# Two prices of a plan, and the order of 531 TensorE tasks, in a float32 attention and mixture-of-experts kernel

## The chip, the cores and the metric

One NeuronCore of one Trainium2 chip. The metric is device time in microseconds (us) of one execution. The kernel before takes 580.03 us, the median of 3 runs (580.02 to 580.44).

## The reference

Eight batches, eight heads, 576 positions, 64 wide: block-causal attention (blocks of 64), its output x goes into four experts, each with its own q, k, v projections (512 to 64) and causal attention, an output projection, and a gate that keeps two of the four.

```python
# attention, per batch and head
scores = q @ k.T / 8;  mask where block(i) < block(j);  attn = softmax(scores);  x = attn @ v
# experts, per batch
logits = x @ w_gate;  w = softmax over the top 2 of 4
for e in range(4):
    q, k, v = x @ wq[e], x @ wk[e], x @ wv[e]
    a = softmax(causal(q @ k.T / 8))
    out += gate[e] * (a @ v @ wo[e])
```

## The kernel before, in words

The work is cut into 48 slots: per batch four pairs of heads of the first attention ("A") and two pairs of experts ("M"), 12.5 us apart in the plan (`TSLOT`). Each slot does for its two heads, with keys and queries on 64 partitions each:

- **scores** (`f_s` in `add_attention`): query tiles of 128 rows against as many keys as the mask lets through, widths 192, 320, 448, 576 (`WID`). `ORDER` groups them in three tasks: the widest tile 3 (with a 64x64 corner), tiles 0 and 1, tile 2. Most are three products of a high and a low part (`hl`, `lo`); tile 0 and the first batch multiply plain float32 (`raw`, `mops`). The tasks of tiles 0, 1 and of tile 2 are called narrow here, that of tile 3 wide.
- row minimum of the negated, masked scores on DVE (`f_m`), exp with a running sum on ACT (`f_e`).
- **transposes** of the exps (`f_t`, 14, 15 or 16 per task), copied from PSUM by ACT or DVE into `eTa` (tiles 0, 1) and `eTb` (tiles 2, 3) (`f_v`).
- **eT times v** (`f_av`, 24 or 32 matmuls as the trace counts them), scaled with the reciprocals of the sums (`f_p1`), split into a high and a low part (`f_p2`, `f_p3`).

Beside the slots stand the **full** products: q and k of the experts (`add_qk`), v (`add_v`), the output projection (`add_out`). On TensorE (PE) these four kinds use the array in three ways. The plan marks each PE task with a mode: F for the full products (128x128), C for eT times v (128x64), S for scores and T for transposes (both 64x128, `TILING` "H").

What sets the order: the kernel does not rely on a scheduler but plans itself (`Plan.run`). Every task has a cost, dependencies and buffers. The plan plays the five queues (PE, ACT, DVE, POOL, SP) forward in its own clock and emits each task when its turn comes. PE's tasks come strictly in the order of the table `LINE`, a permutation of the 531 PE tasks; a task that is not ready keeps PE waiting. The other engines take the ready task with the lowest number in the table `KEYS`, and some tasks (copies, splits) go to whichever of ACT, DVE and POOL is free. `PRICE` is what the plan adds to a PE task when the mode changes ("SF" from S to F), and `c_s` in `add_attention` is what it takes a score task to last. So with a given `LINE` the prices do not order PE; they move the plan's clock of PE, and with it what the other engines find ready.

Of the kernel before, what the change touches and what calls it, by code (L numbers as in the profile page):

```python
# [58 lines left out]
    -61.05, 72.88, -304.49, 285.38, 197.97, 308.44, -90, -485.75, -398.95, -311.49, -310.46, -226.23, -303.95,  # L59
    -200.29, -34.36, -109.87, -30.06, -772.41, 406.92, 36.99, -152.28, -87.06, 7.08, -98.82, 506.04, 1.62, 144.12,  # L60
    -49.87, 59.34, -401.18, 304.55, 589.82, -639.65, -37.72, 51.33, 51.13, 363.43, -16.73, -65.89, 69.77, 71.38,
    -371.59, 575.7, 149.12, -52.5, 104.96, 107.99, -1.27, 338.51, 239.38, -211.47, 124.56, 122.39, -297.31, 280.07,
    443.51, 233.11, 147.49, 81.63, 12.96, 1067.18, 161.48, 784.65, 161.42, 125.87, -195.35, 725.34, 807.9, -217.87,
    164.5, 141.44, 175.16, 781.63, 677.59, 325.44, 163.12, 140.52, 144.51, 440.22, 268.84, -137.83, 201.27, 173.02,
    245.23, 629.28, 442.61, 545.51, 202.32, 269.87, 173.82, 832.33, -48.65, 499.89, 229.38, 195.56, 624.52, 150.18,
    707.74, -57.93, 261.4, 295.79, -255.42, 325.91, 465.42, -305.64, 289.89, 257.36, 257.93, 1202.64, 49.62, 413.63,
    301.23, 296.29, -8.39, 1198.8, 76.81, 224.38, 306.63, 303.26, 535.45, 953.46, 368.95, 582.51, 325.55, 295.98,
    566.34, 713.9, -18.75, -179.96, 357.63, 358.03, 216.69, 733.92, 406.86, 396.51, 391.78, 372.27, -114.52, 562.3,
    652.52, 305.73, 395.02, 342.63, 556.86, 344.09, 662.77, 447.36, 425.58, 400.46, 722.61, 650.31, 592.99, 244.69,
    455.55, 501.82, 523.83, 758.38, 354.59, 317.8, 567.08, 439.03, 70.97, 1094.19, -324.07, 311.7, 595.2, 522.52,  # L70
    314, 531.55, 124.8, 629.88, 471.62, 520.83, 451.03, 1089.28, 1137.64, 795.01, 765.66, 707.37, 477.57, 1225.45,
    -221.62, 764.62, 598.95, -76.75, 113.9, 240.74, -125.38, -108.02, 404.04, 93.98, -349.15, -30.71, -12.22,
    -140.33, -142.11, 6.12, -438.84, -44.69, 364.95, 34.38, 352.96, 61.78, 351.19, 110.73, 5.01, 757.03, -6.95,
    359.21, 201.49, 1.84, -54.25, 483.22, -739.78, -731.32, 7.17, 255.2, -85.56, 415.17, -499.83, 20.32, -281.08,
    186.92, -9.52, -412.56, -28, -25.13, 491.02, 6.62, -368.72, 413.41, 17.8, -980.05, -328.7, -497.05, -449.07,
    69.73, -166.75, -214.9, 26.69, 125.25, 497.09, 242.37, 20.29, 258.64, -36.7, 432.07, 170.76, 11.09, -277.3,
    271.15, -748.81, 581.22, 23.95, 894.06, 241.77, -424.41, -274.26, 36.21, 212.12, -455.4, 231.78, -274.77, 20.91,
    -194.25, 52.79, -25.53, -371.82, 262.65, -26.69, -273.2, -337.99, 142.42, -257.02, 228.08, -130.15, -390.41,
    52.82, 98.9, 885.98, -46.42, 35.39, -29.22, 100.36, -431.26, 404.1, 22.61, -20.89, 71.79, -77.48, 53.08, 24.92,
    548.27, 43.24, -5.98, -509.78, 33.61, 208.79, 192.46, -68.15, 373.75, 7.71, 181.82, -201.58, 31.77, -169.86,  # L80
    348.99, 7.75, 43.39, 264.75, -279.03, 489.2, -193.62, 187.58, 123.51, 52.03, 394.77, -1008.75, -262.95, 58.43,
    -6.54, -604.46, 155.8, -166.41, 32.92, -563.72, -421.41, 295.9, 78.7, 36.85, 695.62, 68.35, 462.77, 504.63,
    32.59, 70.25, 641.61, 219.12, 107.13, 19.31, 131.63, 280.91, 13.26, -242.14, 251.73, 24.01, -717.93, -49.16,
    20.04, -133.98, 215.52, 580.48, -20.65, 59.42, -46.59, 305.54, 243.5, 105.29, -509.23, -516.01, 60.21, -25.78,
    59.3, 358.94, 36.45, -57.58, 74.48, 47.05, 308.04, -206.22, 957.49, 561.1, 64.27, 23.46, 219.54, -583.14,
    -352.66, 33.3, 234.83, -114.24, 35.96, -36.27, 62.05, 66.29, 27.38, -93.48, -671.09, 248.87, -73.25, 180.17,
    -151.19, 82.16, 695.44, 798.54, 364.87, 85.48, 456.72, 301.84, 571.42, 98.78, 69.55, -90.33, 300.55, 18.48,
    1035.48, 22.07, 143.29, 275.43, 196.22, -144.5, 69.53, 503.83, -521.13, 158.9, 520.48, 63.86, 227.15, -629.77,
    25.79, -77.04, 364.92, 49.61, 769.8, 576.6, -693.16, 32.64, -127.69, 345.55, -588.48, 87.18, -233.43, 454.17,
    -515.68, 108.56, -318.55, 263.11, -12.2, 884.88, -43.3, -139.58, 32.01, 277.78, -330.98, -21.7, 567.38, 70.38,  # L90
    8.99, -14.06, 550.12, 90.72, -424.31, -79.85, 75.31, 653.46, 61.48, 364.25, 75.19, 709.07, 76.28, -24.9, 79.85,
    429.96, -603.55, 434.76, 563.52, 346.37, -904.62, -424.27, 217.54, 208.46, -33.4, 323.46, 794.21, 307.74,
    -575.64, -93.77, -160.66, -264.36, -24.47, -372, 593.97, 132.98, -766.42, 80.06, 156.45, 84.68, -5.9, -598.24,
    -67.41, 1106.11, 90.26, -113.18, 83.63, 180.77, 482.69, 99.87, 294.41, 53.86, 149.08, 298.76, -64.86, -891.13,
    81.25, 170.92, -658.3, -250.1, 337.52, 81.14, 602.58, 499.67, 318.97, 487.72, 73.66, 573.01, 415.62, 81.04,
    -71.18, 832.82, 46.33, 255.81, 368.96, -207.19, 51.95, 52.91, 182.3, 159.13, 215.44, 100.54, 286.85, 567.36,
    480.88, 115.39, -433.72, 20.08, -359.31, 81.17, 211.56, -224.8, -265.4, 276.02, 86.93, 588.8, 796.85, 236.19,
    8.45, 93.86, 305.75, 447.42, 506.63, -212.19, 54.29, 198.19, 631.11, 50.3, -339.7, 179.38, 78.24, -43.31,
    -236.77, -530.02, -149.28, 236.07, 446.91, 239.47, 128.01, 104.9, -502.35, 86.41, 111.82, -196.67, 62.74, 34.46,
    -175.69, 97.86, 211.82, 131.16, -117.5, -621.65, 109.31, 310.73, -8.42, -299.88, 614.46, 105.04, 208.76, 828,  # L100
    150.18, -258.73, 96.27, 244.6, 418.51, 60.84, 419.07, -319.32, 104.95, -235.03, 231.9, 555.33, -163.95, -172.06,
    -103.02, -106.94, 139.89, 323.89, -114.19, -336.01, 125.66, -580.49, -690.47, 385.08, -53.84, 115.29, -248.33,
    -1087.38, -27.82, 430.69, 122.89, -244.35, 1060.62, 4.9, 320.44, 125.84, -281.29, -87.32, 704.44, 132.13,
    116.99, -134.72, -527.81, 104.13, -316.36, -254.53, 69.33, 378.26, 89.26, -228.7, 592.26, 360.76, 113.77,
    -177.01, 292.79, 138.4, -717.17, -252.74, 550.47, 143.5, 622.23, 58.38, -301.1, 133.13, -375.99, -24.11, 128.06,
# [182 lines left out]
PRICE = {"FC": 100, "FS": 160, "FT": 85, "CF": 155, "CS": 175, "CT": 148, "SF": 155, "SC": 153, "ST": 0,  # L288
         "TF": 135, "TC": 105, "TS": 8}
# [1072 lines left out]
```

## Time and profile before

| | |
|---|---|
| median of 3 runs | 580.03 us (580.02 to 580.44) |
| profiled execution | 579.71 us, its span 577.9 us |
| PE busy | 566.2 us, 98% of the span |
| DVE, ACT, POOL busy | 467.3, 432.7, 211.0 us (81, 75, 37%) |
| granted TensorE clock | 1.000 |
| DMA | 113 GB/s mean |

The span runs from the first to the last instruction; the profiled execution's own time is 1.8 us longer. "Idle before" is the time in which an engine had nothing running, and what ended it. A busy PE is not the same as a PE at its peak: matmuls are pipelined, and a change of mode lengthens the distance between two tasks without showing as idle time. So the text below measures a PE task by the distance from its first matmul's start to the first start of the next task.

### The profile page before, as it was taken

The numbers are of one execution on the slowest core, as the hardware profiler recorded it, in microseconds if no ns is written. First come the engines' busy times: TensorE is split into PE (matmuls) and PEld (weight loads), VectorE is DVE, ScalarE is ACT, GpSimd is POOL, SyncE is SP. The second block draws the span as 40 slices with busy tenths as digits, with TensorE's granted clock in tenths as the row PEclk, the third lists the DMA queues.
The fourth block names the chain that finished last, engine by engine and source line by source line (L and its number), as shares of the span: only waits on it lengthen the run. The fifth ranks groups of instructions, "written<-read, shape, count | busy, mean of one in ns | idle before, by whom it ended". The sixth has DMA issues, their size and how long they took to land.

```text
span 577.9 us, 19767 instructions
## 1 busy us (share of the span) xinstructions
PE 566.2 (98%) x7794; PEld 525.3 (91%) x7794; DVE 467.3 (81%) x1630; ACT 432.7 (75%) x1363; POOL 211.0 (37%) x330
## 2 busy tenths in 40 slices
PE   7899999999999999999999999999999999999996
PEld 5689999999999989999999999999999999999984
DVE  6999789798978789888877878878898889774851
ACT  5888787888767787677877868768778787665743
POOL 2475236434442253322333516164542434120011
PEclk9999999999999999999999999999999999999999
DMA  6555234322543144422173315343253230301042
GB/s 232 170 197 203 94 123 152 105 67 82 166 163 85 64 121 128 140 83 86 62 240 108 105 41 169 98 143 107 65 183 124 85 105 5 118 4 45 2 173 91
DMA packets 29853, 65.51 MB, mean 113 GB/s; under 512 B 9664, under 2 KB 10176, under 8 KB 29760
## 3 DMA queue, kind: packets, MB, share of 16 engines
q1 hardware_dynamic: 24224, 54.51, 29.6%
q10 hardware_dynamic: 5536, 9.73, 4.8%
q8 instruction: 61, 1.00, 0.7%
q14 instruction: 32, 0.26, 0.2%
HBM read 54.01 MB, written 10.22 MB: 111 GB/s over the span
## 4 chain that ended last, share of the span: by engine, by line
PE 95%; DVE 3%; ACT 1%; issue 0%; POOL 0%; ACTq 0%; DVEq 0%; POOLq 0%
PE bank L325 95%; DVE bank L325 1%; DVE eTb L325 1%; ACT e L325 0%; DVE eTa L325 0%; DVE nm L325 0%; DVE x L325 0%; ACT ob L325 0%; DVE r L325 0%; ACTq L325 0%; POOL id masks.py:199 0%; POOL id masks.py:197 0%; DVE rT L325 0%; DVEq L325 0%; POOLq masks.py:199 0%
## 5 line engine op out<-in xcount | busy, mean ns | idle before, releaser
L325 ACT ACTIVATE e<-bank,nm 128x320 f32<-128x320 f32 (+3 forms) x384 | 218.7, 580 | 27.9 <-DVE nm L325 24.2
L325 DVE CUSTOM_DVE_ANT_0 bank<-bank,mask_a 64x64 f32<-64x64 f32 (+4 forms) x320 | 154.6, 505 | 15.3 <-PE bank L325 8.6
L325 PE MATMUL bank<-x,wh 128*128 128x320 f32 (+1 forms) x512 | 105.7, 301 | 0.0
L325 PEld LDWEIGHTS bank<-id,e 64*128 64x128 f32 x2112 | 86.5, 140 | 14.0 <-issue 5.0
L325 PE MATMUL bank<-id,e 64*128 64x64 f32 x2112 | 96.2, 226 | 1.7 <-ACT e L325 1.6
L325 POOL TENSOR_TENSOR lo<-raw,hl 128x320 fp32r<-128x320 f32 x77 | 65.6, 878 | 78.6 <-ACT hl L325 73.1
L325 PEld LDWEIGHTS bank<-x,wh 128*128 128x128 f32 x512 | 82.0, 188 | 4.0 <-issue 2.7
L325 DVE CUSTOM_DVE_ANT_0 bank<-bank,mask_c 64x64 f32<-64x64 f32 (+4 forms) x160 | 77.4, 506 | 7.3 <-PE bank L325 3.7
L325 PE MATMUL bank<-hl,lo 64*128 64x320 f32 (+2 forms) x352 | 79.9, 380 | 0.4 <-DVE eTb L325 0.4
L325 ACT ACTIVATION_READ_ACCUMULATOR e<-bank,nm 128x1 f32 x384 | 78.5, 204 | 0.0
L325 PE MATMUL bank<-x,wl 128*128 128x256 f32 (+1 forms) x256 | 75.7, 296 | 0.0
L325 ACT COPY eTb<-bank 128x512 f32<-128x512 f32 (+1 forms) x111 | 58.9, 557 | 19.4 <-PE bank L325 18.7
L325 PE MATMUL bank<-hl 64*128 64x320 f32 (+2 forms) x352 | 68.0, 313 | 0.0
L325 PE MATMUL bank<-lo,hl 64*128 64x320 f32 (+2 forms) x352 | 67.7, 313 | 0.0
L325 DVE DVE_READ_ACCUMULATOR2_ANT nm<- 128x1 f32 (+1 forms) x480 | 67.0, 139 | 0.0
L325 PEld LDWEIGHTS bank<-eTb,va 128*64 128x64 f32 x1024 | 59.6, 137 | 3.7 <-issue 2.1
L325 PE MATMUL bank<-eTb,va 128*64 128x128 f32 (+2 forms) x1024 | 62.8, 275 | 0.0
L325 DVE TENSOR_TENSOR x<-bank,rs 128x256 f32<-128x256 f32 (+1 forms) x144 | 46.3, 352 | 17.8 <-PE bank L325 15.1
L325 PE MATMUL bank<-wh,x 128*128 128x260 f32 x288 | 59.2, 289 | 0.0
L325 DVE COPY eTb<-bank 128x512 f32<-128x512 f32 (+1 forms) x81 | 51.7, 654 | 9.2 <-PE bank L325 8.3
L325 PEld LDWEIGHTS bank<-wh,x 128*128 128x128 f32 x288 | 46.9, 188 | 2.9 <-issue 1.4
L325 POOL TENSOR_TENSOR x<-x,x 128x256 fp32r<-128x256 f32 (+1 forms) x43 | 34.9, 814 | 36.8 <-ACT x L325 18.6
(116 smaller groups left out, 1170.4 us busy)
## 6 DMA issues: line engine op xcount, KB each, us to landing
va<-in_v_dram SPq DMA_DIRECT2D x32, 576.0 KB
raw<-in_qk_dram SPq DMA_DIRECT2D x31, 576.0 KB
rs<-dr SPq DMA_DIRECT2D x96, 144.0 KB
out_dram<-ob ACTq DMA_DIRECT2D x32, 256.0 KB
raw<-in_w_dram SPq DMA_DIRECT2D x4, 386.0 KB
out_dram<-ob ACTq DMA_DIRECT2D x8, 128.0 KB
dr<-rT SPq DMA_DIRECT2D x48, 16.0 KB
raw<-in_wo_dram SPq DMA_DIRECT2D x1, 512.0 KB
```

What stands on the lines that cost most here:

```text
L325: r = f(*args, **kwargs)
```

## The change

Both tables are new: `KEYS` (2619 numbers) for the other engines, `LINE` for PE. 269 of the 531 places in `LINE` hold another task than before; of those 148 moved by one place, 67 by two, the farthest by 23. Every task's own instructions are the same, the number of PE instructions too. 79 tasks go from DVE to ACT, 77 from ACT to DVE, 58 from DVE to POOL or back, 37 from ACT to POOL or back; ACT has 730 tasks (721 before), DVE 889 (897), POOL 303 (304).

```diff
 KEYS = [
-    -61.05, 72.88, -304.49, 285.38, 197.97, 308.44, -90, -485.75, -398.95, -311.49, -310.46, -226.23, -303.95,
+    162.95, 160.21, -395.85, 276.68, 82.54, 260.02, -90, -520.61, -409.21, -275.21, -352.21, -239.63, -265.52,
...
 LINE = [
-    0, 2, 1, 3, 4, 12, 5, 11, 6, 10, 7, 20, 9, 18, 15, 19, 13, 14, 8, 23, 22, 28, 26, 21, 16, 27, 17, 25, 31, 30,
+    0, 1, 2, 3, 4, 12, 11, 5, 6, 10, 7, 20, 9, 18, 15, 19, 14, 8, 28, 23, 13, 22, 26, 21, 27, 17, 16, 25, 29, 31,
...
-PRICE = {"FC": 100, "FS": 160, "FT": 85, "CF": 155, "CS": 175, "CT": 148, "SF": 155, "SC": 153, "ST": 0,
+PRICE = {"FC": 100, "FS": 160, "FT": 85, "CF": 155, "CS": 175, "CT": 148, "SF": 200, "SC": 185, "ST": 0,
          "TF": 135, "TC": 105, "TS": 8}
...
             c_s = sum(4 * WID[t] / 2.4 + 10 if hl is None or t == 0 else 3 * (WID[t] / 2.24 + (8 if last else 4)) for t in ts_)
-            c_s += 174 * last + 25 + (32 if ts_[0] == 0 else 18) + 40 * (hl is None)
+            c_s += 174 * last + (25 if last else -20) + (32 if ts_[0] == 0 else 18) + 40 * (hl is None)
```

How often one mode follows another in PE's order, from its 32nd task on (the first 31 are the start, which the prediction takes by itself):

| from, to | F to C | F to S | F to T | C to F | C to S | C to T | S to F | S to C | S to T | T to F | T to C | T to S | no change |
|---|---|---|---|---|---|---|---|---|---|---|---|---|---|
| before | 5 | 3 | 42 | 4 | 12 | 20 | 32 | 15 | 41 | 15 | 16 | 72 | 222 |
| changed | 3 | 5 | 43 | 6 | 14 | 19 | 25 | 14 | 43 | 21 | 22 | 62 | 222 |

All seven of the S to F that are gone left a narrow score task.

Three places. The first is ACT's order in the first pair of heads (exps read a bank, `e_99` is tile 3, `e_97` and `e_98` tile 2 of this pair and the next; numbers are buffers). Before:

```order
6 L325 ACTIVATE el_101,ssum_82<-bank_146,nm 64x64
7 L325 ACTIVATE e_99,ssum_82<-bank_146,nm 128x576
8 L325 ACTIVATE el_101,ssum_82<-bank_147,nm 64x64
9 L325 ACTIVATE e_99,ssum_82<-bank_147,nm 128x576
10 L325 ACTIVATE e_97,ssum_82<-bank_144,nm 128x448 x2
11 L325 ACTIVATE e_98,ssum_83<-bank_145,nm 128x448
12 L325 ACTIVATE r_136<-ssum_82,eps 128x10
13 L325 ACTIVATE e_98,ssum_83<-bank_145,nm 128x448
```

Changed:

```order
8 L325 ACTIVATE el_101,ssum_82<-bank_146,nm 64x64
9 L325 ACTIVATE e_99,ssum_82<-bank_146,nm 128x576
10 L325 ACTIVATE e_97,ssum_82<-bank_144,nm 128x448
11 L325 ACTIVATE e_97,ssum_82<-bank_145,nm 128x448
12 L325 ACTIVATE e_98,ssum_83<-bank_144,nm 128x448
13 L325 ACTIVATE e_98,ssum_83<-bank_145,nm 128x448
14 L325 ACTIVATE el_101,ssum_82<-bank_147,nm 64x64
15 L325 ACTIVATE e_99,ssum_82<-bank_147,nm 128x576
16 L325 ACTIVATE r_136<-ssum_82,eps 128x10
```

The second head's exp of tile 3 now stands behind four exps of width 448, where it stood before them. DVE's minima change in the same way.

The second is PE's order at the same place (`raw_73` and `raw_74` are q and k of the first two pairs, `id` marks transposes). Before:

```order
8 L325 MATMUL bank_146<-raw_73 128x64
9 L325 MATMUL bank_147<-raw_73 128x64
10 L325 MATMUL bank_144<-raw_73 128x448 x2
11 L325 MATMUL bank_145<-raw_74 128x448 x2
12 L325 MATMUL bank_146<-id_65,e_99 128x64 x16
13 L325 MATMUL bank_147<-raw_74 128x192 x2
14 L325 MATMUL bank_147<-raw_74 128x320 x2
15 L325 MATMUL bank_144<-id_65,e_95 128x64 x4
```

Changed:

```order
12 L325 MATMUL bank_144<-raw_73 128x448
13 L325 MATMUL bank_145<-raw_73 128x448
14 L325 MATMUL bank_144<-raw_74 128x448
15 L325 MATMUL bank_145<-raw_74 128x448
16 L325 MATMUL bank_146<-raw_74 128x192 x2
17 L325 MATMUL bank_146<-raw_74 128x320 x2
18 L325 MATMUL bank_144<-id_65,e_99 128x64 x16
19 L325 MATMUL bank_145<-id_65,e_95 128x64 x4
```

The scores of the next pair's tiles 0 and 1 (`raw_74`, widths 192 and 320) now come ahead of the 16 transposes of `e_99` instead of behind them.

The third is PE's order in the middle of the program (tasks 232 to 236 of 531): the end of a wide score task, a narrow one of width 448 (`hl_77`), and eT times v (`eTa`, `eTb`). Before:

```order
2183 L325 MATMUL bank_147<-raw_74 128x64
2184 L325 MATMUL bank_144<-raw_74 128x64
2185 L325 MATMUL bank_145<-hl_77,lo_79 128x448
2186 L325 MATMUL bank_146<-hl_77,lo_79 128x448
2187 L325 MATMUL bank_145<-hl_77 128x448
2188 L325 MATMUL bank_146<-hl_77 128x448
2189 L325 MATMUL bank_145<-lo_79,hl_77 128x448
2190 L325 MATMUL bank_146<-lo_79,hl_77 128x448
2191 L325 MATMUL bank_146<-eTa_104,vz 64x64 x2
2192 L325 MATMUL bank_146<-eTa_104,vm 64x256
2193 L325 MATMUL bank_146<-eTa_104,vm 64x2x64
```

Changed:

```order
2214 L325 MATMUL bank_146<-raw_75 128x64
2215 L325 MATMUL bank_147<-raw_75 128x64
2216 L325 MATMUL bank_145<-id_65,e_99 128x64 x16
2217 L325 MATMUL bank_144<-eTa_103,vz 64x64 x2
2218 L325 MATMUL bank_144<-eTa_103,vm 64x256
2219 L325 MATMUL bank_144<-eTa_103,vm 64x2x64
2220 L325 MATMUL bank_144<-eTa_103,vm 64x64
2221 L325 MATMUL bank_144<-eTa_103,vz 64x2x64
2222 L325 MATMUL bank_144<-eTa_103,vm 64x128
2223 L325 MATMUL bank_144<-eTa_103,vz 64x64 x5
2224 L325 MATMUL bank_144<-hl_77,lo_79 128x448
2225 L325 MATMUL bank_145<-hl_77,lo_79 128x448
```

Before, the narrow scores followed the wide ones and then came both products with v. Now 16 transposes follow the wide scores (they stood ahead of them), and the narrow scores stand between the two products with v: C to S and S to C once more, S to S and C to C once less.

## Rows read from the trace of the kernel before

**Rows 1.** the page: busy time, share of the span and number of instructions by engine; the shares of the chain that ended last.

```profile
PE 566.2 (98%) x7794; PEld 525.3 (91%) x7794; DVE 467.3 (81%) x1630; ACT 432.7 (75%) x1363; POOL 211.0 (37%) x330
...
PE 95%; DVE 3%; ACT 1%; issue 0%; POOL 0%; ACTq 0%; DVEq 0%; POOLq 0%
```

**Rows 2.** busy time by engine in stretches of the execution: start and end, length, then for each engine its busy time and its instructions, the granted TensorE clock in parts of full speed, DMA share, GB/s.

```profile
40.00:300.00 260.00, 259.97 (x3646) 243.74 (x3644) 222.24 (x775) 203.05 (x643) 104.02 (x160) 1.00 0.36 118
300.00:560.00 260.00, 260.00 (x3574) 243.87 (x3572) 208.71 (x725) 193.88 (x612) 86.85 (x133) 1.00 0.30 93
```

**Rows 3.** who waited for whom, PE's rows alone, from 0 to 40 us: total wait, times, longest. (From 40 us to the end the same view has no row for PE.)

```profile
PE bank L325 <- ACT e L325: 2.8, 5, 1.1
PE bank L325 <- POOL id masks.py:199: 1.4, 1, 1.4
```

**Rows 4.** timeline of PE, 424.5 to 440 us (start, length, engine, line, operation, out<-in, tile, count; in brackets idle time before): the first row of each of some tasks and the row that begins the next.

```profile
427.10 0.39 PE L325 MATMUL bank<-woh,y 128*128 128x512 f32 x1
...
428.49 0.28 PE L325 MATMUL bank<-wh,x 128*128 128x260 f32 x1
...
430.79 0.59 PE L325 MATMUL bank<-id,e 64*128 64x64 f32 x11
...
431.19 0.46 PE L325 MATMUL bank<-hl,lo 64*128 64x448 f32 x1
...
433.70 0.40 PE L325 MATMUL bank<-woh,y 128*128 128x512 f32 x1
...
435.18 0.41 PE L325 MATMUL bank<-hl,lo 64*128 64x320 f32 x2
...
438.64 1.22 PE L325 MATMUL bank<-eTa,va 128*64 128x64 f32 x24
439.79 0.40 PE L325 MATMUL bank<-id,e 64*128 64x64 f32 x6
```

**Rows 5.** timeline of PE, 474 to 484.8 us, same columns.

```profile
478.82 0.22 PE L325 MATMUL bank<-eTa,va 128*64 128x64 f32 x1
...
479.82 0.22 PE L325 MATMUL bank<-eTa,vz 128*64 128x64 f32 x1
...
483.19 0.36 PE L325 MATMUL bank<-hl,lo 64*128 64x448 f32 x1
...
483.80 0.55 PE L325 MATMUL bank<-hl,lo 64*128 64x448 f32 x2
...
484.68 0.41 PE L325 MATMUL bank<-x,wh 128*128 128x320 f32 x1
```

**Rows 6.** timeline of PE, 490.4 to 503.9 us, same columns.

```profile
497.83 0.44 PE L325 MATMUL bank<-hl,lo 64*128 64x448 f32 x1
...
498.51 0.48 PE L325 MATMUL bank<-mops 64*128 64x192 f32 x3
...
499.27 0.54 PE L325 MATMUL bank<-id,e 64*128 64x64 f32 x10
...
499.98 0.50 PE L325 MATMUL bank<-woh,y 128*128 128x512 f32 x1
...
501.47 0.28 PE L325 MATMUL bank<-wh,x 128*128 128x260 f32 x1
```

**Rows 7.** timeline of PE, 392.4 to 395.8 us, same columns.

```profile
393.24 0.50 PE L325 MATMUL bank<-hl,lo 64*128 64x448 f32 x2
...
393.85 0.54 PE L325 MATMUL bank<-id,e 64*128 64x64 f32 x10
...
394.57 0.33 PE L325 MATMUL bank<-eTa,vz 128*64 128x64 f32 x4
...
395.62 0.41 PE L325 MATMUL bank<-eTb,vm 128*64 128x256 f32 x3
```

**Rows 8.** timeline of PE, 83 to 84 us, same columns.

```profile
83.35 0.54 PE L325 MATMUL bank<-id,e 64*128 64x64 f32 x12
...
83.94 0.41 PE L325 MATMUL bank<-x,wh 128*128 128x320 f32 x1
```

**Rows 9.** timeline of PE, 341.3 to 343 us and 528.9 to 532 us, same columns.

```profile
341.47 0.59 PE L325 MATMUL bank<-id,e 64*128 64x64 f32 x12
...
341.93 0.39 PE L325 MATMUL bank<-hl,lo 64*128 64x320 f32 x1
...
529.70 0.47 PE L325 MATMUL bank<-hl,lo 64*128 64x448 f32 x2
...
530.41 0.31 PE L325 MATMUL bank<-hl,lo 64*128 64x320 f32 x2
```

**Rows 10.** timeline of ACT and PE in the first attention pair, 0 to 20 us, same columns.

```profile
10.14 0.31 ACT L325 ACTIVATE el<-bank,nm 64x64 f32<-64x64 f32 x1
...
11.16 0.62 ACT L325 ACTIVATE e<-bank,nm 128x448 f32<-128x448 f32 x1
...
11.31 0.72 PE L325 MATMUL bank<-id,e 64*128 64x64 f32 x16 [0.99 <-ACT e L325]
...
11.77 0.62 ACT L325 ACTIVATE e<-bank,nm 128x448 f32<-128x448 f32 x1
...
11.87 1.08 PE L325 MATMUL bank<-raw 64*128 64x192 f32 x8
...
12.79 0.54 PE L325 MATMUL bank<-id,e 64*128 64x64 f32 x12
```

426 rows, old and new, of tables (KEYS, LINE) are left out of this document.

## The prediction

> **What bounds the kernel.** I read the page first: PE is busy 98% of the span, and the chain that ended last lies on PE for 95% of it [rows 1]. Then the busy times by stretch: from 40 to 560 us PE is never without work (519.97 of 520 us) at the full granted clock, while DVE and ACT are at 75 to 85% [rows 2]. Then who waited for whom: PE waits only in the first 40 us, 6.3 us in all by that view, of which 1.4 us is the wait for the identity matrix and 2.8 us for exps [rows 3]. So past the start no transfer and no other engine sets the pace, and PE's work does not change: the same tasks with the same instructions. What can change there is the distance between tasks where the mode changes. The last views are therefore PE's timeline at such places [rows 4 to 9] and the start [rows 10].
>
> **What a change of mode costs.** I take the distance from a task's first matmul to the next task's first, for one kind of task in different company, and split each price into what the task that leaves is lengthened by and what the task that enters is.
>
> - F: an output projection between two F tasks lasts 1.39 us (427.10 to 428.49) [rows 4]. Ahead of scores it lasts 1.48 (433.70 to 435.18) [rows 4]: leaving costs 0.09. Behind transposes 1.49 (499.98 to 501.47) [rows 6]: entering costs 0.10.
> - T: 15 transposes between two score tasks last 0.40 (430.79 to 431.19) [rows 4]. Ahead of F or C 0.71 [rows 6] and 0.72 [rows 7], but also 0.59 (83.35 to 83.94) [rows 8]: leaving costs 0.19 to 0.32, and I take 0.25, the middle. Behind F 0.46 [rows 9]: entering costs 0.06; behind C the same is assumed.
> - S: a score task of width 448 between two S lasts 0.61 (483.19 to 483.80), ahead of F 0.88 [rows 5]: leaving costs 0.27, and to C the same is assumed. Ahead of T 0.61 (393.24 to 393.85) [rows 7]: free. Behind T 0.68 [rows 6]: entering 0.07. Behind F 0.71 [rows 9]: 0.10, from C the same.
> - C: 24 products with v between C tasks last 1.00 [rows 5], behind T 1.05 [rows 7], ahead of T 1.15 [rows 4]: entering 0.05, leaving 0.15.
>
> The sums of leaving and entering: S to F 0.37, S to C 0.32, T to F 0.35, T to C 0.30, F to S 0.19, F to T 0.15, C to S 0.25, C to T 0.21, C to F 0.25, F to C 0.14, T to S 0.07, S to T 0.
>
> **What the new order adds from the 32nd PE task on** (the table of the change, changed minus before): S to F -7, that is -2.59 us; S to C -1, -0.32; F to C -2, -0.28; C to T -1, -0.21; T to S -10, -0.70. Against it T to F +6, +2.10; T to C +6, +1.80; C to S +2, +0.50; C to F +2, +0.50; F to S +2, +0.38; F to T +1, +0.15. Together +1.33 us. The new prices make leaving S dearer in the plan, and the order does leave from T instead, but the trace gives T nearly the same price, and four more stretches of S and T are opened and closed. The uncertain piece is T's leaving: at 0.19 on all twelve the sum is +0.6, at 0.32 it is +2.1. The third place of the order is one such case: products with v cut in two by a narrow score task.
>
> The rule of the Trainium skill for this, page "TensorEngine Tiling (Array Packing)", section "Key Properties" under "Tiling Modes", is that changing the tiling mode drains TensorE, while another tile in the same mode does not. By it all changes between F, C and S or T would cost alike and T to S nothing; that is the fourth rival below. The trace agrees that T to S is nearly free, and not that the others are equal: 0.14 to 0.37 us.
>
> **The start.** ACT takes the second head's exp of tile 3 after four exps of width 448 instead of before. Such an exp takes 0.61 us of ACT (11.16 to 11.77), so it begins 2.4 us later than at 10.14, and the 16 transposes that wait for it, at 11.31 before with 0.99 us of idle PE ahead of them, would come at about 13.7 [rows 10]. Into that wait PE now puts the next pair's scores of tiles 0 and 1, 0.92 us (11.87 to 12.79) [rows 10]. So the 15 transposes behind begin at 13.7 + 0.6 = 14.3 in place of 12.79: +1.5 us. What is late next are the copies of those transposes, and the next scores that need their banks. Much of the delay is given back, since of PE's waits some 3.3 us still follow in the start (6.3 less 1.4, 0.99 and 0.6 for a transfer), and in each of them a late PE waits less: ACT paces this stretch, and its exps are the same. I take +0.2 us; bounds +1.5 (nothing given back) and -1.0 (the wait of 0.99 is filled and the exp is not late).
>
> **At nothing.** The moves between ACT, DVE and POOL (ACT nine tasks more, DVE eight fewer, POOL one fewer): covered by PE, which never waits for them past 40 us [rows 2, 3]; if the cover is gone, see the fifth rival. SP's queue: loads of v change places at the start, with the products that use them in nearly the same places on PE; no PE wait on a load of v is in the trace, and a late one would be part of the +1.5 above. The end: the last copies and stores on ACT are in the same order, and only two half projections of PE's last three change places: nothing.
>
> **Sum.** 1.33 + 0.2, about +1.5 us. The profiled execution took 579.71 us, with a span of 577.9 and 1.8 around it, which I leave as it is; it lies 0.32 below the median of the runs. The sum put on the execution gives 581.2, on the median 580.03, which is what will be compared, **581.5 us**. Its own range, with T's price and some of the start, is 580.4 to 582.4.
>
> **Rivals.** I call no change what is within 0.2%, 1.16 us, about what a measurement of this kernel can tell.
>
> 1. The forecast, +1.5 us: chance 0.38.
> 2. Faster: the start. PE loses 4.9 us there after the identity. If the new order fills the 0.99 us and half of the other 3.9, it gains 2.9 us, and with +1.3 for the modes the time is 578.4. It decides from a gain of 2.5 us in the start. For it: all of PE's idle time that an order can still win lies there, and scores are indeed put into the wait. Against it: the exp that is waited for is put off by 2.4 us. Chance 0.22.
> 3. The change does not do what its prices say: T is as cheap to leave as the cheap rows (0.19), the start comes out even, +0.6 us, 580.6: no change. For it: 0.59 [rows 8] is as real as 0.71. Chance 0.20.
> 4. Each change of tiling costs the same. From the 32nd task on there are 172 of them instead of 164; the mean of the prices above over the 164 is 0.26 us, so +2.1, and with the start 582.3. Against it: leaving C or F is cheaper than leaving S or T in the rows. Chance 0.12.
> 5. New waits in the middle: a transpose task moved ahead meets an exp that is not there yet. PE's waits for exps in the start are 2.8 us in five, 0.6 each [rows 3]; three such give +1.8 on top, 583.3. Against it: before has none in 520 us with ACT and DVE this busy [rows 2]. Chance 0.08.
>
> **How the numbers follow.** The forecast's range falls on both sides of +1.16: of its 0.38, 0.25 is slower and 0.13 no change. Rivals 4 and 5 are slower (0.20), rival 3 is no change but for 0.02 on either side (0.16), rival 2 is faster but for 0.01. So slower 0.47, no change 0.30, faster 0.23. The range from 578.5 to 583.4 leaves out about half of rival 2 and half of rival 5, with a little beyond: under 2 in 10.
>
> **What would show it.** Right: from 40 us on PE has no idle time as before, yet it needs over a microsecond more for the same tasks; tasks of transposes ahead of F or C last 0.6 to 0.7 us, and there are more of them; the 16 transposes of the first tile 3 begin near 13.7 us with over 2 us of idle PE ahead, and by the 32nd task the delay is a few tenths. Wrong: PE's total wait in the first 40 us well below 6.3 us (rival 2); a PE row in the waits after 40 us (rival 5); transposes ahead of F or C mostly at 0.6 us (rival 3).

## The result, and the profile after

The changed kernel takes 583.56 us, the median of 6 runs (582.95 to 586.59), against 580.02 (579.23 to 580.49, 6 runs) for the kernel before: a ratio of 1.0074, 95% interval 1.0049 to 1.0100. That is 3.5 us slower where 1.5 was forecast, and just outside the range (583.4). The profiled execution took 583.92 us, its span is 582.1 us. All of the 4.2 us between the spans can be followed on PE, task by task, because both orders hold the same tasks. One execution below, of the kernel with the prices alone, was slow (713.59 us at a granted clock of 0.725) and is left out of its figures.

PE's waits from 0 to 40 us in the profile after, against [rows 3]:

```profile
PE bank L325 <- ACT e L325: 3.7, 4, 2.3
PE bank L325 <- POOL id masks.py:199: 2.1, 1, 2.1
PE bank L325 <- DVE eTb L325: 0.6, 1, 0.6
PE bank L325 <- ACT eTb L325: 0.2, 1, 0.2
```

The sum is hardly larger (6.6 us, before 6.3), but it lies in other places: 0.7 more for the identity and one wait of 2.3 for an exp. The stretches of [rows 2], after:

```profile
40.00:300.00 260.00, 258.52 (x3608) 243.38 (x3605) 219.32 (x766) 203.48 (x644) 107.21 (x162) 1.00 0.36 117
300.00:560.00 260.00, 259.77 (x3599) 243.50 (x3598) 210.60 (x736) 194.83 (x611) 86.48 (x134) 1.00 0.29 92
```

Past 40 us PE now has 1.48 us of idle time in one place and 0.2 in another, where it had none. PE's timeline in the start and at that place (idle time before in brackets), against [rows 10]:

```profile
10.62 1.13 PE L325 MATMUL bank<-raw 64*128 64x192 f32 x8 [0.84 <-ACT e L325]
14.08 1.63 PE L325 MATMUL bank<-id,e 64*128 64x64 f32 x28 [2.33 <-ACT e L325]
...
15.95 2.26 PE L325 MATMUL bank<-raw 64*128 64x320 f32 x12
...
19.76 2.00 PE L325 MATMUL bank<-eTb,va 128*64 128x256 f32 x32 [0.25 <-ACT eTb L325]
...
41.95 0.41 PE L325 MATMUL bank<-hl,lo 64*128 64x320 f32 x2 [1.48 <-DVE eTa L325]
```

The 16 transposes of the first tile 3 start at 14.08 (before: 11.31) behind 2.33 us of idle PE, as the prediction said. What it did not say stands in the granted clock, the third column from the right in this view by stretches of 1 us:

```profile
13.00:14.00 1.00, 0.00 (x0) 0.00 (x0) 0.93 (x5) 1.00 (x5) 0.92 (x2) 1.00 0.00 0
14.00:15.00 1.00, 0.92 (x20) 0.92 (x22) 0.93 (x6) 0.33 (x2) 1.00 (x2) 0.65 0.00 0
15.00:16.00 1.00, 0.97 (x19) 0.82 (x15) 0.78 (x3) 0.62 (x2) 0.61 (x1) 0.50 0.02 8
...
18.00:19.00 1.00, 1.00 (x24) 0.79 (x20) 0.72 (x3) 0.58 (x3) 0.00 (x0) 1.00 0.30 113
```

Behind the wait PE runs at half its clock (1.2 GHz) from 14.3 to 17.7 us: the 12 score matmuls take 2.26 us instead of 1.41. And ACT, which the prediction took for the engine that paces this stretch and loses nothing, now stands still until those late transposes are done. Its timeline after:

```profile
13.19 0.74 ACT L325 ACTIVATE e<-bank,nm 128x576 f32<-128x576 f32 x1
...
15.11 0.58 ACT L325 COPY eTb<-bank 128x512 f32<-128x512 f32 x1 [0.74 <-PE bank L325]
15.96 0.53 ACT L325 COPY eTa<-bank 128x448 f32<-128x448 f32 x1 [0.27 <-PE bank L325]
16.39 0.43 ACT L325 ACTIVATE e<-bank,nm 128x192 f32<-128x192 f32 x1
```

The minimum for the exp at 16.39 was done at 13.68, but in ACT's order two copies of transposes stand ahead of it. From 10 to 20 us ACT is busy for 8.54 us (before 9.87) and DVE for 7.95 (9.76).

The wait at 41.95 has its origin on SP and DVE. The issues on SP, then DVE at the place:

```profile
33.31 0.33 SPq L325 DMA_DIRECT2D raw<-in_w_dram  x1
33.74 1.10 SPq L325 DMA_DIRECT2D rs<-dr  x2
```

```profile
40.85 0.42 DVE L325 TENSOR_TENSOR x<-bank,rs 128x256 f32<-128x256 f32 x1 [1.47 <-DMA rs<-dr]
41.20 0.61 DVE L325 COPY eTa<-bank 128x448 f32<-128x448 f32 x1
```

The reciprocals' load (144 KB), which before was issued at 31.81 and ahead of the experts' weights (386 KB), now goes behind them and lands at 40.8. DVE waits for it, and the copy into `eTa` that frees PE's bank stands behind that. By the trace's semaphore records, which hold when the parts of a transfer have landed, the second half of this load lands 6.5 us after its issue (34.26 to 40.76); in before it took 3.2 (32.33 to 35.52).

Where the time is lost: the starts, in us, of the 16 transposes and of five PE tasks, and the end of PE's last matmul. Ahead of each of these five tasks both orders have done the same set of tasks, so that their starts can be compared (the expectations count from 0 and call the 44th task the 43rd). "Rest" is from the 44th task to the end without the idle time in it. The rows below the second are the experiments, in their order; each is one profiled execution.

| run | 16 transposes | 16th | 23rd | 32nd | 33rd | 44th | PE's end | idle behind 44th | rest |
|---|---|---|---|---|---|---|---|---|---|
| before | 11.31 | 22.32 | 28.45 | 37.95 | 39.34 | 52.03 | 572.52 | 0.03 | 520.46 |
| after | 14.08 | 23.47 | 30.44 | 39.43 | 41.95 | 54.63 | 576.75 | 0.23 | 521.89 |
| as after, written out | 13.17 | 23.40 | 30.36 | 39.36 | 41.39 | 54.08 | 575.80 | 0.01 | 521.71 |
| before's start | 10.84 | 21.85 | 27.98 | 37.48 | 38.87 | 51.98 | 574.38 | 0.35 | 522.05 |
| changed start | 13.08 | 23.30 | 30.26 | 39.25 | 40.28 | 52.98 | 574.25 | 0.41 | 520.86 |
| identity first | 13.30 | 23.65 | 30.61 | 39.60 | 40.63 | 53.58 | 575.27 | 0.02 | 521.67 |
| exp early | 11.37 | 22.15 | 29.88 | 40.45 | 42.14 | 54.81 | 577.15 | 0.43 | 521.91 |
| copy first | 13.19 | 23.41 | 30.37 | 39.38 | 40.41 | 53.56 | 576.00 | 0.49 | 521.95 |
| reciprocals first | 13.19 | 23.42 | 30.38 | 39.37 | 40.40 | 53.64 | 575.66 | 0.24 | 521.78 |
| scores repeated | 13.25 | 23.85 | 30.82 | 39.81 | 40.94 | 53.62 | 575.29 | 0.02 | 521.65 |
| PE kept busy | 13.28 | 21.63 | 29.60 | 40.18 | 41.21 | 53.91 | 575.71 | 0.04 | 521.76 |
| three moves | 11.22 | 22.29 | 30.01 | 38.99 | 40.02 | 53.16 | 574.98 | 0.01 | 521.81 |
| prices only | 12.22 | 24.35 | 32.09 | 41.56 | 42.46 | 62.73 | 590.85 | 4.59 | 523.53 |
| more mode changes | 10.76 | 21.76 | 27.89 | 37.39 | 38.78 | 51.46 | 582.25 | 3.71 | 527.08 |

So the loss of the start comes in two pieces. At the 32nd task the changed kernel is 1.48 us behind (39.43 against 37.95), and the wait at the 33rd (1.48 us, before 0.35) adds 1.13.

### The profile page after: what moved, and what is told of

Its sections match the earlier page's. It is cut to its first block, busy times and chain, and to the rows that moved or that the text cites. A ratio compares the mean times of both kernels' runs of the same rounds, so it can differ in the third digit from the quotient of the medians.

```text
span 582.1 us, 19790 instructions
## 1 busy us (share of the span) xinstructions
PE 568.3 (98%) x7794; PEld 527.5 (91%) x7794; DVE 462.7 (79%) x1624; ACT 436.0 (75%) x1371; POOL 211.9 (36%) x328
## 4 chain that ended last, share of the span: by engine, by line
PE 93%; DMA 3%; DVE 2%; ACT 1%; issue 0%; POOL 0%; SPq 0%; ACTq 0%; POOLq 0%; DVEq 0%
PE bank L325 93%; DMA rs<-dr 2%; DVE bank L325 1%; DMA dr<-rT 1%; ACT e L325 1%; DVE eTb L325 0%; DVE eTa L325 0%; ACT ob L325 0%; DVE x L325 0%; ACT eTb L325 0%; SPq L325 0%; DVE nm L325 0%; POOL mask_a L325 0%; ACT el L325 0%; ACTq L325 0%
## 5 line engine op out<-in xcount | busy, mean ns | idle before, releaser
L325 DVE CUSTOM_DVE_ANT_0 bank<-bank,mask_a 128x192 f32<-128x192 f32 (+4 forms) x320 | 154.5, 505 | 18.6 <-PE bank L325 11.9
L325 POOL TENSOR_TENSOR lo<-raw,hl 128x320 fp32r<-128x320 f32 x72 | 62.1, 887 | 61.1 <-ACT hl L325 32.6
L325 DVE CUSTOM_DVE_ANT_0 bank<-bank,mask_c 128x320 f32<-128x320 f32 (+4 forms) x160 | 77.5, 506 | 7.4 <-PE bank L325 4.3
L325 PE MATMUL bank<-hl,lo 64*128 64x320 f32 (+2 forms) x352 | 77.9, 379 | 1.5 <-DVE eTa L325 1.5
L325 ACT COPY eTb<-bank 128x512 f32<-128x512 f32 (+1 forms) x117 | 61.4, 555 | 20.3 <-PE bank L325 19.6
L325 PE MATMUL bank<-x,wl 128*128 128x320 f32 (+1 forms) x256 | 75.5, 295 | 0.0
L325 PE MATMUL bank<-hl 64*128 64x320 f32 (+2 forms) x352 | 66.0, 313 | 0.0
L325 PE MATMUL bank<-lo,hl 64*128 64x320 f32 (+2 forms) x352 | 65.7, 313 | 0.0
L325 DVE COPY eTb<-bank 128x512 f32<-128x512 f32 (+1 forms) x75 | 48.4, 661 | 10.1 <-PE bank L325 9.1
L325 POOL TENSOR_TENSOR lo<-mops,hl 128x192 fp32r<-128x192 f32 (+1 forms) x48 | 32.2, 697 | 46.2 <-ACT hl L325 33.8
```

The source lines that it names most:

```text
L325: r = f(*args, **kwargs)
```

## The experiments

Theory "start": most of the excess over the forecast is lost in the start. Its rival "middle" puts it into the new order behind the start. In most of these kernels the order of ACT, DVE, POOL and SP is a list too (written out from the plan's own result), so that an edit moves what it names and nothing else:

```diff
                     if e == "P" and line:
...
+                    elif e != "P":
+                        n_ = ticks[e]
+                        t = self.tasks[ORDER_OF[e][n_]] if n_ < len(ORDER_OF[e]) else None
+                        q = [(t.key, t.seq, t)] if t and t.put else []
```

**Nothing moved** (the measure for the others).

> The changed kernel with all five queues written out as its plan sets them, nothing moved: the measure for the other runs, on the same chip. Both theories: the changed kernel's time, 583.2 to 584.0, runs spread over about 3.5 us, some with a PE wait of over 1 us at the 33rd task and some without.

Measured: 582.99 us (582.75 to 584.38), before 580.17; ratio 1.0057 (1.0045 to 1.0070), inside the changed kernel's interval, its median 0.2 below what was expected. Its profile has the idle 2.33 us, the low clock (12.5 to 19.3 us) and 0.99 us of idle PE at the 33rd task.

**Before's start, changed rest.**

```diff
-LINE, ORDER_OF: the changed order
+LINE, ORDER_OF: what before's plan emits ahead of PE's 44th task, then the rest in the changed order
```

> The changed kernel with the start of the kernel before: all that the plan emits ahead of PE's 43rd task stands in before's order, the rest in the changed order. All five queues are written out, so nothing else moves. Theory 'start': of the 4.2 us between the two profiled spans, 2.6 are lost by PE's 43rd task (54.63 against 52.03 us) and 1.6 behind it. Then this takes 2.6 less than the changed kernel, about 581.0, PE's waits past 43 us stay at 0.2 and the 43rd PE task starts at 52.0. Rival 'middle': what is lost in the start would have been given back or lost again anyway; then it stays within 0.8 us of the changed kernel, 582.8 to 583.6. Rival 'handover': the new order behind meets the old start with new waits; then it is above 584 and PE rows after 43 us show it.

Measured: 582.58 (581.56 to 582.95), before 580.17; 1.0041 (1.0029 to 1.0053). In the trace the start's 2.6 us are gone (51.98), and 0.35 us of idle PE come in soon behind the place where the parts meet. The profiled run is 2.4 us faster than the changed kernel's, the medians differ by 1.0 (0.4 to the run with nothing moved, which was on another chip; the kernel before has the same median, 580.17, on both): between the theories. The rest, 522.05, is the changed order's.

**The counterpart: changed start, before's rest.**

```diff
-LINE, ORDER_OF: before's order
+LINE, ORDER_OF: what the changed plan emits ahead of PE's 44th task, then the rest in before's order
```

> The counterpart of the run with before's start: the kernel before with all that the changed plan emits ahead of PE's 43rd task in the changed order, the rest as before, all queues written out. Theory 'start': the start alone costs 2.6 us at the 43rd PE task (54.6 against 52.0 us) and the middle, being before's, gives nothing back: about 582.8, and the runs spread over 3 to 4 us as the changed kernel's do. Rival 'middle': the start's delay is made good, and the loss is the new order behind it: 580.2 to 581.0. Rival 'both less': with medians the start was worth 1.0 (583.56 against 582.58 with before's start): 581.2.

Measured: 582.79 (581.43 to 584.70), before 580.43; 1.0042 (1.0028 to 1.0057), as "start" said, 2.4 us slower, with the spread. The profiled run is the shortest of the eight (581.43): 0.95 lost at the 44th task, without the wait at the 33rd. Its rest, 520.86, is close to before's. So by the medians the start costs about 2.4 us by itself, the rest as much by itself, and together they cost 2.8 to 3.5. The two do not add up; whether a part of each is hidden when both are there, or the spread of the runs makes it so, is not shown.

**Identity first.**

```diff
 ORDER_OF["G"]
-    1, 0, 5, ...
+    0, 1, 5, ...
```

> The changed kernel, all queues written out, with two neighbours on POOL changed: the identity matrix ahead of the mask's memsets, as in before. Theory 'passed on': PE's first task starts at 1.35 instead of 2.07 us, and since the first scores follow it directly, 0.72 us are passed on up to the first wait; behind it the exps on ACT pace the start, which begin with the first scores, so all of it comes through: 0.5 to 0.7 us less, about 582.9. Rival 'load': the first scores wait for their load instead of the identity, and nothing is gained: within 0.2 us.

Measured: 583.65 (582.38 to 586.41); 1.0067 (1.0045 to 1.0090): nothing gained. PE's first task starts 0.72 earlier, at 1.35, but the scores of the 7th at 9.65, where they start at 9.71 with nothing moved: the first scores start at 3.95 (nothing moved: 4.51), and the 7th task waits 0.70 us for an exp. The theory was wrong, and its rival right in the size, though the wait is for an exp and not for a load.

**Exp early.**

```diff
 ORDER_OF["A"]
-    ... 217, 222, 224, 260, 262, 219, ...
+    ... 217, 219, 222, 224, 260, 262, ...
```

(and the same on DVE for its minimum.)

> The changed kernel, all queues written out, with one pair of moves: the second head's minimum (DVE) and exp (ACT) of tile 3 go ahead of the four of width 448, as in before. Theory 'late exp': the 16 transposes start at about 11.8 instead of 14.08, PE's wait of 2.33 us is gone, no wait in the first 20 us is above about 1.1 us, and the granted clock stays at 1.00 there, as in before. PE's 32nd task starts 0.5 to 1.5 us earlier and the time is about 582.3. Rival 'ACT paces': the four exps come 1.1 us later each and the next transposes wait for them instead; the sum of PE's waits in the start stays within 0.5 us and the time within 0.5 us of the changed kernel. On the clock: if it falls all the same, the wait of 2.33 was not what it followed.

Measured: 585.30 (584.34 to 585.63); 1.0082 (1.0068 to 1.0096), the slowest of the single moves. The transposes start at 11.37, but the next waits take all of it:

```profile
12.60 0.59 PE L438 MATMUL bank<-id,e 64*128 64x64 f32 x12 [0.51 <-ACT e L438]
15.49 1.41 PE L438 MATMUL bank<-raw 64*128 64x320 f32 x12 [2.17 <-DVE eTb L438]
...
29.88 1.76 PE L438 MATMUL bank<-raw 64*128 64x320 f32 x12 [1.48 <-ACT e L438]
```

"ACT paces" is right in its kind: PE's idle time ahead of the 44th task is 8.5 us, 8.2 in the profile after, in other places. The time is 1.7 us above the changed kernel's, where it gave 0.5. On the clock: it stays at 1.00 through the idle 2.17 us, and falls behind the 1.48 at 29.88 (0.50 from 31 to 34 us).

**Copy first**, and **reciprocals first**: two ways to take away the wait at 41.95.

```diff
 ORDER_OF["D"]
-    ... 341, 320, 343, ...
+    ... 341, 343, 320, ...
```

> The changed kernel, all queues written out, with two neighbours on DVE changed: the copy of the transposes into eTa goes ahead of the scaling by the reciprocals that waits for a transfer until 40.8 us. Theory 'behind a transfer': PE's wait of 1.48 us at 41.95 is only that copy standing behind the waiting scaling; then PE starts that task at about 40.5, as far behind before as it was at its 31st task (1.5 us), and the time falls by 1.1 to 1.5 us, to about 582.3. Rival 'the next one waits': the late transfer holds another task that PE needs (the scaled x, or the bank that the scaling reads), and PE's wait only moves to a later task: within 0.4 us of the changed kernel.

```diff
 ORDER_OF["S"]
-    ... 313, 196, 314, ...
+    ... 313, 314, 196, ...
```

> The changed kernel, all queues written out, with two neighbours on SP changed: the load of the reciprocals (144 KB) goes ahead of the experts' weights (386 KB) that were issued 0.4 us before it. Theory 'behind the weights': the reciprocals land several us earlier, the scaling on DVE does not wait until 40.8 us, PE's wait of 1.48 us at 41.95 is gone as in the run with the copy first, and so is the long tail of the runs (585.65 and 586.59): 582.9 to 583.4, none above 585. Rival 'round trip': the reciprocals are late because their own write to memory lands late; the wait stays, and the tail too.

Measured: 583.31 (582.88 to 584.67), 1.0058 (1.0046 to 1.0070), and 584.06 (582.73 to 585.12), 1.0070 (1.0057 to 1.0084). PE does not wait at the 33rd task in either, but it does not in the runs with the changed start and with the identity first either, and 0.09 us in the one with repeated scores: the wait comes and goes by the execution, and its absence alone shows nothing. The semaphore records do. With the reciprocals first, their second half lands 3.2 us after its issue (34.11 to 37.30), as in before; behind the weights it takes 4.6 to 6.5 us, in after and the eight other profiled runs with the changed start. So the load is late because it goes behind the weights, and by how much depends on the execution. Neither edit makes the kernel faster: at the 33rd task they are 1.0 us ahead of the run with nothing moved, at the 44th 0.4 to 0.5, since waits of 0.25 and 0.33 us at tasks between took a part, and the long runs are still there (584.67 and 585.12, where none above 585 was expected of the second).

**Scores repeated** and **PE kept busy**: is it the clock?

```diff
-            def f_s(e, ts_=ts_, sbs=sbs, view=view, last=last):
-                for t in ts_ + ((-1,) if last else ()):
+            def f_s(e, ts_=ts_, sbs=sbs, view=view, last=last, again=3 if len(plan.tasks) == 253 else 1):
+                for t in (ts_ + ((-1,) if last else ())) * again:
```

> The changed kernel, all queues written out as they are; the one difference is that the PE task ahead of the 2.33 us wait (scores of the next pair's tiles 0 and 1, 1.13 us) multiplies the same products three times, the last of which stands. Theory 'clock': the granted clock of 0.5 from 14.6 to 17.5 us follows the idle PE and lengthens what runs in it (28 transposes 1.63 us, 12 score matmuls 2.26 instead of 1.41). With PE busy to 14 us the clock stays at 1.00, the tile-2 scores that started at 18.40 start about 1.3 us earlier, and the end comes 0.4 to 1.3 us earlier, since later waits in the start take part of it back; the spread of the runs (3.6 us) shrinks towards before's (1.3). Rival 'no clock': the low clock has another cause, it falls all the same and the time is that of the changed kernel or up to 1 us more by the later minima.

Measured: 582.44 (581.52 to 583.36); 1.0041 (1.0028 to 1.0053). The wait of 2.33 is gone, but the later minima delay a copy, PE waits 0.60 and then 1.33 us, and the clock falls behind that (0.51 in 16 to 17 us): inconclusive on the clock. The other kernel:

```diff
+    def keep_busy(e):
+        for _ in range(9):
+            nc.tensor.matmul(bank(kb)[:, 0:P], lhsT=id32, rhs=id32, start=True, stop=True)
+    plan.add("P", 9 * 250, keep_busy, 0, deps=(ident,), get=(kb,), rel=(kb,))
```

> The changed kernel, all queues written out, with nine products of the identity with itself (0.25 us each as in the first task) into a bank that is free, on PE between the scores of tiles 0 and 1 and the 16 transposes that wait 2.33 us for the late exp. Nothing reads them, and no other task's order or wait changes. Theory 'clock': it is the idle PE that the clock of 0.5 follows; kept busy, PE stays at 1.00 from 10 to 30 us and does the five tasks behind about 1.3 us faster. Most of that is given back in the next waits (before has 0.56 and 1.05 us of idle PE at the same tasks), so PE's 32nd task starts only 0 to 0.7 us earlier and the time is 582.8 to 583.5. Rival 'clock sets the start': the low clock is what the start lost, and the time falls by 1.3 us or more, to 582.2 or less. Rival 'other cause': the clock falls with PE busy too.

Measured: 584.08 (582.51 to 586.46); 1.0076 (1.0057 to 1.0096). PE and the clock in it:

```profile
10.00:20.00 10.00, 9.31 (x121) 7.53 (x120) 8.62 (x32) 9.48 (x34) 2.82 (x3) 1.00 0.28 80
```

```profile
14.96 1.41 PE L440 MATMUL bank<-raw 64*128 64x320 f32 x12 [0.47 <-DVE eTb L440]
...
17.93 2.00 PE L440 MATMUL bank<-eTb,va 128*64 128x256 f32 x32
...
29.60 1.77 PE L440 MATMUL bank<-raw 64*128 64x320 f32 x6 [1.70 <-DVE eTa L440]
```

In this stretch the clock stays at 1.00 and the products with v start at 17.93 instead of 19.76: 1.8 us won, and with it the whole delay of the late exp: the 16th task starts at 21.63, in before at 22.32 and in the run with before's start at 21.85. At the 23rd task PE waits 1.70 us for a copy on DVE, the clock falls there instead (0.5 from 29.7 to 33.2 us), and at the 44th task 0.17 us are left against nothing moved. So the low clock follows the idle PE here, and without it the delay is made good by the 16th task. It is not the whole loss: at 27.90, still at full clock, PE has done the same 22 tasks that before has done at 28.45, and then waits until 29.60. The time met neither theory (582.8 to 583.5, and 582.2 or less).

**Three moves together**: the diffs of identity first, exp early and copy first in one kernel.

> The changed kernel, all queues written out, with the three moves together: identity ahead of the mask on POOL, the second head's minimum and exp of tile 3 ahead of the four of width 448, the copy into eTa ahead of the scaling on DVE. Theory 'start': these three places are what the start lost, so the loss up to PE's 43rd task is 0 to 0.5 us against before instead of 2.6, the rest (1.4 of mode changes, 0.2 of a wait) stays: 581.5 to 582.2, with a spread of runs like before's. Rival 'order of the start': the exps and scores in their new places cost by themselves; then 582.5 or more.

Measured: 583.50 (582.18 to 584.27); 1.0051 (1.0037 to 1.0065): the rival. The three places are not all that the start lost: 53.16 at the 44th task, 1.13 behind before, with waits of 2.46 us at the 10th and 1.47 at the 23rd. Here the clock stays at 1.00 from 7.2 us to PE's end, so this loss holds no low clock. Behind the first wait:

```profile
14.00:15.00 1.00, 0.00 (x0) 0.00 (x0) 0.94 (x5) 1.00 (x5) 1.00 (x2) 1.00 0.00 0
15.00:16.00 1.00, 0.38 (x3) 0.36 (x5) 1.00 (x2) 1.00 (x7) 0.52 (x1) 1.00 0.03 8
16.00:17.00 1.00, 1.00 (x18) 0.95 (x15) 0.07 (x1) 0.52 (x3) 0.00 (x0) 1.00 0.16 33
```

**Prices only**: the last two hunks of the change on before's tables.

```diff
-PRICE = {... "SF": 155, "SC": 153, ...
+PRICE = {... "SF": 200, "SC": 185, ...
...
-            c_s += 174 * last + 25 + ...
+            c_s += 174 * last + (25 if last else -20) + ...
```

> The kernel before with its own two tables, and only the new prices (S to F 200, S to C 185, narrow scores 45 less). PE's order is before's, place by place; the other engines' order and 119 assignments move because the plan's clock does. In the start ACT takes the second head's exp of tile 3 behind two of the four of width 448, with PE's transposes still right behind its scores. Theory 'PE hides it': past 40 us nothing waits, as before; only the start shows: the 16 transposes wait 1.2 us longer (0.99 becomes 2.2), the clock may fall as in the changed kernel, and the time is 580.5 to 582. Rival 'cover': with other engines at 75 to 85% a new order among them makes PE wait in the middle: rows for PE after 43 us, and 582 or more. Rival 'nothing': 580.2.

Measured: 597.03 us (595.62 to 598.70, 5 runs), before 580.43; 1.0283 (1.0263 to 1.0303). PE's waits from 43 us on:

```profile
PE bank L325 <- POOL x L325: 3.6, 1, 3.6
PE bank L325 <- DVE ytl L325: 1.6, 2, 0.9
PE bank L325 <- ACT eTa L325: 1.5, 2, 1.1
PE bank L325 <- ACT e L325: 1.2, 2, 0.6
PE bank L325 <- ACT eTb L325: 0.8, 1, 0.8
```

PE's order is before's, place by place, and the kernel is 16.6 us slower. "Cover" is right, and by far more than it gave. Of the 18.3 us between the ends of PE 10.7 are lost ahead of the 44th task (62.73; the wait of 3.6 us and a low clock from 53.9 to 60.7 us lie there), 7.6 behind it. What the prediction costed at nothing, the moves of the other engines, is not free by itself: with before's `KEYS` and `LINE` and the new prices PE waits for POOL, DVE and ACT past 43 us; with the `KEYS` and `LINE` of the change it does so for 0.2 us.

**More mode changes** (68 places of PE's order on before's queues).

```diff
-LINE = before's
+LINE = 68 places between 66 and 482 hold a task from up to a few places away
```

> The kernel before, all five queues written out as its plan sets them, with 68 places of PE's order between the 66th and the 482nd task holding a neighbour's task, so that the mode changes oftener: S to F +4, S to C +8, T to F +5, F to S +8, C to S +6, C to T +3, C to F -1, T to S -2; changes of tiling 197 instead of 164. Start, the other queues and their engines are before's. What PE loses from its 60th task on without idle time: by the prediction's row prices 9.05 us; by a fit of the same prices to all distances of before, the changed kernel and the run with before's start 7.7; by one price for each change of tiling (0.26 x 33) 8.6; by the new prices in the plan 5.6; by a theory that modes are not what the middle loses, 0 to 2. Moved tasks can meet banks or exps that are late: up to 1.7 us of idle PE on top, shown as waits. The time: 588.5 to 591 by the row prices, 587.5 to 589.5 by the fit, 585.5 to 587.5 by the plan's.

Measured: 591.03 (589.45 to 591.86), before 579.68; 1.0190 (1.0174 to 1.0206). From the 60th task to the end PE loses 10.3 us, of which 3.7 us are idle (1.8 for a load of v); 6.6 us are lost without idle time, at a clock of 1.00. Mode changes do cost in the middle. The size lies between the plan's prices (5.6) and the fit (7.7); the prediction's rows (9.05) are a third too dear here, and so is one price for all changes (8.6).

## Why the prediction was wrong

1. **What bounds the kernel: right.** Past the 44th task PE has 0.01 to 0.5 us of idle time in all runs but the two that disturb the plan, and the order of its modes sets the rest.
2. **The price of the modes: right in the sum, in part by luck.** Forecast +1.33; the trace shows +1.43 without idle time (521.89 less 520.46), the runs with the same order +1.2 to +1.6. The run with before's order there and the changed start shows +0.40 too, so a few tenths of it need not be the modes. By the drain rule of the Trainium skill ("TensorEngine Tiling (Array Packing)", "Key Properties" under "Tiling Modes"), read as one price, it would have been +2.1; the trace does not agree with one price. Transposes do leave dearly: behind narrow scores a task of 15 takes 0.67 us on the mean ahead of F and 0.69 ahead of C (0.58 to 0.72), and 0.40 to 0.45 ahead of scores. But the prices together were too high, which the sum hid: they gave 9.05 for the run with more mode changes, which lost 6.6. At the third place of the change, after and then before:

```profile
254.93 0.41 PE L325 MATMUL bank<-hl,lo 64*128 64x320 f32 x2
...
256.00 0.66 PE L325 MATMUL bank<-id,e 64*128 64x64 f32 x16
256.59 0.34 PE L325 MATMUL bank<-eTa,vz 128*64 128x64 f32 x4
...
257.76 0.47 PE L325 MATMUL bank<-hl,lo 64*128 64x448 f32 x2
...
258.57 1.08 PE L325 MATMUL bank<-eTb,vm 128*64 128x256 f32 x12
```

```profile
252.38 0.71 PE L325 MATMUL bank<-id,e 64*128 64x64 f32 x16
252.88 0.42 PE L325 MATMUL bank<-hl,lo 64*128 64x320 f32 x2
```

   The 16 transposes leave for C after 0.59 us, against 0.50 ahead of scores in before: 0.09, not 0.25. From the two full products ahead of this place to the second product with v, the same six tasks in both orders take 0.20 us more than before (6.54, 252.03 to 258.57, against 6.34, 249.41 to 255.75); the prices give 0.52.
3. **The start: wrong, and this is the step that failed.** "Much of the delay is given back ... ACT paces this stretch, and its exps are the same. I take +0.2 us; bounds +1.5 ... and -1.0." The exp is late as worked out (14.08, forecast 13.7), with the idle PE as forecast. But at the 32nd task, where "a few tenths" were to be left, PE is 1.48 us behind, as if nothing had been given back; at the 44th it is 2.60 behind, over the bound (2.05 with nothing moved; 0.95 in the profile of the changed start alone, whose median is 2.4 behind at the end). The runs show three things in the place of that step.
   - The low clock, a term that the sum did not have. In the one run that keeps the exp late and PE busy, so that the clock stays up, the delay is given back as forecast: none of it is left at the 16th task, where after is 1.15 behind.
   - The engines that pace come later themselves. The 23rd task, scores that wait for exps and copies, starts without a wait at 28.45 in before; in all ten profiled runs with the changed start it waits 0.57 to 1.70 us and starts at 29.60 at the earliest, whatever PE did ahead of it. ACT and DVE do their tasks in a fixed order: the late transposes hold the copies, the copies hold exps that are ready, and from 10 to 20 us ACT is busy for 1.3 us less and DVE for 1.8. "Its exps are the same" is true of their number, not of their times.
   - The load of the reciprocals at the 33rd task, +1.13 us in after, which the prediction had put at nothing (below).

   How the loss divides between the three is not shown, since the same start left PE's 44th task at 54.63, 54.08 and 52.98 us in three profiled executions. The six single edits (53.6 to 54.8) lie within that, or just above it, so none of them shows a gain; only before's whole start reaches 52.0.
4. **At nothing: half wrong.** POOL's moves were covered "by PE, which never waits for them past 40 us", but the mask's two memsets went ahead of the identity, and PE's first task waits for it: 0.72 us, to be seen in the first two numbers of the diff (162.95 and 160.21, before -61.05 and 72.88). Undoing it gained nothing. Of SP's queue the prediction named the loads of v alone; the load of the reciprocals behind the weights makes PE wait 0.7 to 1.5 us at the 33rd task in three of the ten profiled runs with the changed start.
5. **The rivals.** The fifth (new waits) came nearest in time, 583.3, by luck: it meant transposes that wait for exps in the middle, where there is one wait of 0.2 us; the wait at 42 us is for a load. The second (faster by the start) named the place and had the sign wrong.

What stays open: the run with before's start gains 2.4 us in its profile and 0.4 to 1.0 in the medians; the runs of all kernels with the changed start spread over up to 4 us, and one profile each does not show what the longer ones do.

## What to carry to other kernels

Where several engines work almost without a pause in fixed orders (ACT and DVE in before, busy for 9.9 and 9.8 us from 10 to 20 us), a wait in the new order need not end when it did in the old one: follow a late task to what stands behind it on each queue, and to that engine's next ready task, before calling it absorbed. A repair of one wait in such a stretch is worth what the next wait leaves of it: here, six times, nothing beyond the spread of the runs. A table of priorities belongs to the costs that it was made for: here the new costs with the old table took 16.6 us.

## What was not expected of the hardware

The low clock followed an idle PE, but not each time. During or just behind 2.2 to 2.5 us of idle time it fell in six profiled runs (after, nothing moved, copy first, reciprocals first, identity first, changed start) and in the one with prices only, and stayed at 1.00 in two (2.17 and 2.46 us). Of idle times between 1.3 and 2 us three were followed by it (1.33, 1.48, 1.70) and four were not (1.47, 1.48 at 41.95 in after, 1.79, 1.91). It stayed low for 3.4 to 6.8 us. Before's longest idle time past the identity, 1.05 us, was never followed by it, there or in the run with before's start.

The first score tasks differ between executions with nothing else changed: the 4th PE task (the first scores of tile 3, two heads) takes 1.69 us in the profile after and 1.14 with nothing moved. That moves the start by up to 0.9 us from one run to another (the 7th task at 10.62 and 9.71). The trace's own records of the clock say why: they begin, with 1.00, at 7.47 us in the profile after and at 5.64 with nothing moved, and the views print 1.00 ahead of that too, where there is no record. Pairs of scores with 320 columns follow each other every 0.53 us ahead of that time (5.84, 6.37, 6.91 in after) and every 0.27 us behind it (6.01, 6.28, 6.55 with nothing moved), as at the lower and the upper of the two levels. In before's profile the record begins at 7.51, in the run with before's start at 5.41, and its 16th task starts 0.5 us earlier (21.85 against 22.32). The Trainium skill ("TensorE: Matmul & The Clock Gate", Part 1) says that TensorE starts at the lower clock and that the point of its rise varies; the trace agrees, with a rise between 5.4 and 7.5 us.
